# Summing phi(k) over the tiles by strided reductions on the Vector engine instead of column-tiled matmuls

## The chip, the cores and the metric

The kernel runs on one core of a Trainium2 chip. The metric is the device time of one execution in microseconds (us). A profile is one execution taken by the hardware profiler; its span is about 2 us shorter than the time. TensorE (PE) does the matmuls, PEld is its weight load, DVE is the Vector engine, ACT the Scalar engine, POOL GpSimd. The granted clock is the share of TensorE's full clock that the throttle let through.

## The reference, cut to what matters

```python
phi = lambda t: jnp.where(t > 0, t + 1, jnp.exp(t)) + 1e-6
pq, pk = phi(q), phi(k)
kv = jnp.einsum("bhsd,bhse->bhde", pk, v)
z = jnp.einsum("bhsd->bhd", pk)                       # sum over all 2048 rows
num = jnp.einsum("bhqd,bhde->bhqe", pq, kv)
den = jnp.einsum("bhqd,bhd->bhq", pq, z)[..., None] + 1e-6
a = (num / den) ... @ wo                              # linear attention, 32 heads of 16
b = mixer_mlp(x)                                      # layernorm, two large matmuls with gelu
out = g * a + (1 - g) * b                             # g: a sigmoid gate per row
```

The change is about `z`, the sum of phi(k) over all rows, which the normalizer `den` needs. phi(k) lies in `pk`, 128 partitions by 16 tiles by 512 channels, bf16. Its 2048 rows are 16 tiles of 128 partitions, so `z` is a sum over the 16 tiles and then over the partitions.

## The kernel before

The sum over the tiles was sixteen matmuls, each 32 columns wide, accumulated in PSUM, issued between steps of another accumulation (`gacc`). Two ops on DVE then split the sum into two bf16 parts, and four small matmuls summed over the partitions.

```python
def z_tile(t):
    g = t % 4
    mm(zacc[32 * g : 32 * g + 32, :], zsel[:], pk[:, t, :], t < 4, t >= NT - 4,
       tile_position=(0, 32 * g))
...
zacc = bank("zacc")
for t in range(NT - LAG, NT):
    g_tile(t)
    if t == NT - 3:
        for u in range(NT):
            z_tile(u)
...
nc.vector.tensor_copy(out=zhi[:], in_=zacc[:])
nc.vector.scalar_tensor_tensor(out=zhl[:], in0=zhi[:], scalar=odd[:], in1=zacc[:], ...)
```

Then come the query steps. Each has three matmuls of the MLP (`uacc`), four of a query block (`qacc`), and on DVE two ops that make phi(q) (`pqT`). After them TensorE works through the other eleven MLP tiles of sixteen matmuls each (j = 3 to 13). In between stand the normalizer's matmuls (`den_matmuls`), and the chain that multiplies `pqT` by one over the denominator (`rden`), 16 multiplications on DVE fed by DMA:

```python
for j in range(NB0, NF):                 # NB0 = 3, NF = 14
    ...                                  # sixteen uacc matmuls, gelu
    if j == NB0:
        den_matmuls()
        rden_chain()
    elif j <= NB0 + ND:
        w2_matmul(j - NB0 - 1)
    ...
```

The output phase follows: for each of 16 tiles four `aps` matmuls and fourteen `yps` matmuls.

## Time and profile before

| | before |
|---|---|
| time, median of 3 runs | 168.21 us (167.87 to 168.40) |
| span of the profile | 166.4 us |
| TensorE busy, granted clock | 97%, 0.998 |
| DVE busy | 48% |

The first lines are from the page: busy times with their share of the span and the instructions, and then the span in 40 slices of 4.2 us, each digit the busy share of one slice in tenths (9 is 90% or more); PEclk is the granted clock in the same tenths.

```profile
PE 161.7 (97%) x806; PEld 74.9 (45%) x806; DVE 80.2 (48%) x190; ACT 59.0 (35%) x91; POOL 18.2 (11%) x37
...
PE   7999999999999999999999999999999999999992
...
PEclk9999999999999999999999999999999999999999
```

The next is the chain of work that ended last, by engine:

```profile
PE 94%; DMA 3%; DVE 1%; SPq 0%; issue 0%
```

TensorE's last wait, 0.41 us for a DMA, ends at 6.03 us, and nearly the whole chain is TensorE's. The time is the length of its instruction stream. Now the timeline of TensorE around the sums (start, duration, engine, line, op, out<-in, shape, count), and after the query steps:

```profile
30.24 2.75 PE L109 MATMUL gacc<-pk,xs 128*128 128x512 bf16 x12
32.92 1.05 PE L109 MATMUL zacc<-pk,zsel 128*32 128x512 bf16 x16
33.91 1.90 PE L109 MATMUL gacc<-pk,xs 128*128 128x512 bf16 x8
35.64 0.60 PE L109 MATMUL uacc<-hs,w1c 128*128 128x512 bf16 x2
```

```profile
60.87 3.62 PE L109 MATMUL uacc<-hs,w1c 128*128 128x512 bf16 x16
64.41 1.05 PE L109 MATMUL denps<-pqT,Z 128*32 128x512 bf16 x16
```

From start to start, the sums and the last gacc steps fill 30.24 to 35.64 us. An MLP tile with the tiling switch after it takes 64.41 - 60.87 = 3.54 us.

DVE in one query step (the bracket is the idle time in front and what ended it):

```profile
52.63 0.29 DVE L208 TENSOR_SCALAR e<-e 128x512 bf16<-128x512 bf16 x1 [0.49 <-ACT e L207]
52.96 0.69 DVE L211 SCALAR_TENSOR_TENSOR pqT<-qacc,e 128x512 bf16<-128x512 f32 x1
54.14 0.29 DVE L208 TENSOR_SCALAR e<-e 128x512 bf16<-128x512 bf16 x1 [0.49 <-ACT e L207]
```

A step comes every 1.51 us; DVE works for about one of it and waits 0.49 us for ACT. This looks like room for a reduction of half a microsecond or a little more.

### The profile page before, as it was taken

The page shows a single profiled execution, that of the slowest core. Times are in us where ns is not written, and L with a number is a line of the kernel's source. Part 1 is how long each engine was busy: PE and PEld are TensorE (multiplying, and loading weights), DVE is VectorE, ACT ScalarE, POOL GpSimd, SP SyncE. Part 2 cuts the span into 40 slices and gives each one's busy share as a digit, 9 for nine tenths or more (in the row PEclk, how much of TensorE's full clock was granted, in tenths as well). Part 3 has the DMA queues.
Part 4 walks back from the last instruction along what each step waited for, and adds up shares of the span by engine and source line. Part 5 has one row for each costly group of instructions (what it writes and reads, how often), then busy time and mean ns, then how long its engine had stood idle before and what let it go on. Part 6 is the DMA issues. An engine that isn't in the chain of part 4 may idle for free.

```text
span 166.4 us, 2105 instructions
## 1 busy us (share of the span) xinstructions
PE 161.7 (97%) x806; PEld 74.9 (45%) x806; DVE 80.2 (48%) x190; ACT 59.0 (35%) x91; POOL 18.2 (11%) x37
## 2 busy tenths in 40 slices
PE   7999999999999999999999999999999999999992
PEld 3544444444544444444444444444444444444461
DVE  1569999986986769992301504051222121111121
ACT  3272474827658557222222111051111222111110
POOL 5000602100020000002712521000000000000000
PEclk9999999999999999999999999999999999999999
DMA  5999999999700001910597499931100000110001
GB/s 155 257 181 274 345 352 347 348 349 338 186 0 2 0 0 55 357 33 32 188 293 194 140 336 274 313 127 64 35 32 32 32 33 32 47 51 32 32 32 32
DMA packets 28953, 24.78 MB, mean 149 GB/s; under 512 B 6736, under 2 KB 28368, under 8 KB 28944
## 3 DMA queue, kind: packets, MB, share of 16 engines
q1 hardware_dynamic: 26928, 21.76, 45.0%
q0 software_dynamic: 1440, 2.38, 5.0%
q10 hardware_dynamic: 576, 0.52, 1.0%
q8 instruction: 6, 0.10, 0.3%
q14 instruction: 3, 0.02, 0.0%
HBM read 21.11 MB, written 2.23 MB: 140 GB/s over the span
## 4 chain that ended last, share of the span: by engine, by line
PE 94%; DMA 3%; DVE 1%; SPq 0%; issue 0%
PE uacc L109 29%; PE yps L109 29%; PE gacc L109 8%; PE qacc L109 8%; PE aps L109 8%; PE kacc L109 8%; DMA wk_sb<-in_A_wqkv_dram 3%; PE zacc L109 1%; PE denps L109 1%; PE kvps L109 1%; PE wps L109 1%; SPq L125 0%; DVE ot L471 0%; PE pt L197 0%; DVE xT L203 0%
## 5 line engine op out<-in xcount | busy, mean ns | idle before, releaser
L109 PE MATMUL uacc<-hs,w1c 128*128 128x512 bf16 x224 | 52.0, 379 | 0.0
L109 PE MATMUL yps<-uT,w2c 128*128 128x512 bf16 (+1 forms) x238 | 51.0, 367 | 0.0
L109 PEld LDWEIGHTS <-w2c 128*128 128x128 bf16 x238 | 23.3, 98 | 25.3
L109 PEld LDWEIGHTS <-w1c 128*128 128x128 bf16 x224 | 21.7, 98 | 26.3 <-issue 0.4
L471 DVE SCALAR_TENSOR_TENSOR ot<-yps,c,a_sc 128x512 bf16<-128x512 f32 (+1 forms) x17 | 12.1, 719 | 42.2 <-PE yps L109 41.2
L456 ACT ACTIVATE a_sc<-aps,c,gg 128x512 f32<-128x512 f32 x16 | 12.3, 777 | 46.8 <-PE aps L109 38.9
L418 DVE TENSOR_TENSOR pqT<-pqT,rex 128x512 bf16<-128x512 bf16 x16 | 6.6, 425 | 26.6 <-DMA rex<-rd_dram 26.5
L337 ACT ACTIVATE uT<-uacc,bcol 128x512 bf16<-128x512 f32 x14 | 9.3, 687 | 27.5 <-PE uacc L109 27.5
L109 PE MATMUL kacc<-wk_sb,xT 128*128 128x512 bf16 x64 | 16.1, 379 | 0.5 <-DMA wk_sb<-in_A_wqkv_dram 0.4
L109 PE MATMUL aps<-W2sb,pqT 128*128 128x512 bf16 x64 | 16.4, 379 | 0.0
L109 PE MATMUL qacc<-xT,wq_sb 128*128 128x512 bf16 x64 | 16.4, 379 | 0.0
L109 PE MATMUL gacc<-pk,xs 128*128 128x512 bf16 x64 | 16.1, 380 | 0.0
L247 ACT ACTIVATE hs<-xs,nmr,rstd 128x512 bf16<-128x512 bf16 x16 | 12.8, 804 | 2.5 <-DVE nmr L241 2.5
L207 ACT ACTIVATE e<-qacc 128x512 bf16<-128x512 f32 x16 | 9.6, 597 | 10.2 <-PE qacc L109 10.2
L207 ACT ACTIVATE e<-kacc 128x512 bf16<-128x512 f32 x16 | 9.1, 593 | 8.9 <-PE kacc L109 8.9
L208 DVE TENSOR_SCALAR e<-e 128x512 bf16<-128x512 bf16 x32 | 9.1, 284 | 6.3 <-ACT e L207 6.3
L211 DVE SCALAR_TENSOR_TENSOR pk<-kacc,e 128x512 bf16<-128x512 f32 x16 | 11.1, 692 | 0.6
L211 DVE SCALAR_TENSOR_TENSOR pqT<-qacc,e 128x512 bf16<-128x512 f32 x16 | 11.1, 692 | 0.5
L416 POOL DMA_DIRECT2D rex<-rd_dram x16 | 9.4, 597 | 16.6 <-DVE pqT L418 14.9
L231 DVE BATCH_NORM_STATS2 stats<-xs 128x6 f32<-128x512 bf16 x16 | 10.9, 682 | 0.0
L404 DVE CUSTOM_DVE_ANT_0 junk<-xs,gw_b 128x512 bf16<-128x512 bf16 x16 | 9.9, 688 | 0.0
L109 PEld LDWEIGHTS <-xT 128*128 128x128 bf16 x64 | 6.1, 98 | 8.2 <-issue 0.9
(66 smaller groups left out, 67.6 us busy)
## 6 DMA issues: line engine op xcount, KB each, us to landing
w2c<-in_B_w_dram SPq DMA_DIRECT2D x4, 1792.0 KB, 9.8
w1c<-in_B_w_dram SPq DMA_DIRECT2D x2, 2048.0 KB, 16.1
w1c<-in_B_w_dram SPq DMA_DIRECT2D x3, 1024.0 KB, 11.3
rex<-rd_dram POOLq DMA_DIRECT2D x16, 128.0 KB, 6.6
out_dram<-ot SPq DMA_DIRECT2D x15, 128.0 KB, 1.7
xs<-in_A_x_dram SPq DMA_DIRECT2D x2, 512.0 KB, 4.0
xs<-in_A_x_dram SPq DMA_DIRECT2D x2, 256.0 KB, 4.4
wq_sb<-in_A_wqkv_dram SPq DMA_DIRECT2D x1, 512.0 KB, 6.0
```

What stands on the lines that cost most here:

```text
L109: nc.tensor.matmul(o, lhsT=lhsT, rhs=rhs, start=start, stop=stop, **kw)
L207: nc.scalar.activation(out=e[:], in_=acc[:], func=ACT.Exp)
L208: nc.vector.tensor_scalar(out=e[:], in0=e[:], scalar1=1.0, scalar2=PHI_EPS, op0=ALU.min, op1=ALU.add)
L211: nc.vector.scalar_tensor_tensor(out=dst, in0=acc[:], scalar=0.0, in1=e[:], op0=ALU.max, op1=ALU.add)
L231: nc.vector.bn_stats(out=stats[:], in_=xs[:, t, :])
L247: nc.scalar.activation(out=hs[:, t, :], in_=xs[:, t, :], func=ACT.Identity, scale=rstd[:, t : t + 1], bias=nmr[:, t : t + 1],)
L337: nc.scalar.activation(out=uT[:, j, :], in_=acc[:], func=ACT.Gelu_apprx_tanh, bias=bcol[:, j : j + 1])
L404: nc.vector.tensor_tensor_reduce(out=junk[:], in0=xs[:, t, :], in1=gw_b[:], scale=1.0, scalar=0.0, op0=ALU.mult, op1=ALU.add, accum_out=gp ...
L416: nc.gpsimd.dma_start(out=rex[:], in_=src.unsqueeze(1).to_broadcast([8, HEAD, SC]))
L418: nc.vector.tensor_tensor(out=seg, in0=seg, in1=rex[:], op=ALU.mult)
L456: nc.scalar.activation(out=a_sc[:], in_=aps[:], func=ACT.Identity, scale=gg[:, t : t + 1], bias=c2[:, t : t + 1],)
L471: nc.vector.scalar_tensor_tensor(out=ot[:, :W], in0=yps[:, :W], scalar=c1[:, t : t + 1], in1=a_sc[:, cs], op0=ALU.mult, op1=ALU.add,)
```

## The change

Its intent is to take the sixteen matmuls off the engine that bounds the kernel and put the sum on DVE, which has time. Sixteen reductions each sum 32 channels over the 16 tiles. Ten stand in query steps 6 to 15, six after them. As the sum is ready later, the matmuls of the normalizer go two MLP tiles later.

```diff
-    def z_tile(t): ...                       # sixteen column-tiled matmuls
+    def z_sum(i):
+        d = slice(i * 32, (i + 1) * 32)
+        nc.vector.tensor_reduce(
+            out=zacc[:, d], in_=pk[:, :, d].rearrange("p t d -> p d t"), op=ALU.add, axis=AX.X
+        )
 ...
+    def z_split():
+        nc.vector.tensor_copy(out=zhi[:], in_=zacc[:])
+        nc.vector.tensor_tensor(out=zlo[:], in0=zacc[:], in1=zhi[:], op=ALU.subtract)
+    def z_matmuls(): ...                     # eight small matmuls (zps) instead of four, then Z32
 ...                                          # in the query steps:
+        if t >= 6:
+            z_sum(t - 6)
 ...                                          # after them:
+    for i in range(10, 16):
+        z_sum(i)
+    z_split()
 ...                                          # in the MLP tiles:
-        if j == NB0:
-            den_matmuls()
-            rden_chain()
-        elif j <= NB0 + ND:
-            w2_matmul(j - NB0 - 1)
+        if j == NB0 + 1:
+            z_matmuls()
+        if j == NB0 + 2:
+            den_matmuls()
+            gate_sums()                      # 16 DVE ops, before: in front of the reciprocal
+            rden_chain()
+        if NB0 + 3 <= j < NB0 + 3 + ND:
+            w2_matmul(j - NB0 - 3)
```

The innermost dimension of each reduction's input is `t`, so two elements that are read one after the other lie 512 bf16 values, 1024 bytes, apart.

More of the change, by code (lines that the diff above doesn't have):

```diff
@@ L83 @@
     zhi = keep([P, D], BF16, "zhi")
-    zhl = keep([P, D], BF16, "zhl")
-    odd = keep([P, 1], FP32, "odd")
-    neg8 = keep([P, 8], BF16, "neg8")
-    zsel = keep([P, 32], BF16, "zsel")
+    zlo = keep([P, D], BF16, "zlo")
+    zacc = keep([P, D], FP32, "zacc")
+    ones8 = nc.const_aps.tensor(1.0, (P, 8), BF16)
     rden = keep([P, SC], BF16, "rden")
@@ L162 @@
     nc.vector.memset(Z32[:], 0.0)
-    nc.vector.memset(zsel[:], 0.0)
-    nc.vector.memset(zsel[:, 0:2], 1.0)
-    nc.vector.memset(neg8[:], -1.0)
     nc.gpsimd.memset(ident[:], 0.0)
@@ L170 @@
     )
-    nc.vector.tensor_reduce(out=odd[:], in_=ident[:, 1:P:32], op=ALU.add, axis=AX.X)
     block_mask(mask[:].rearrange("p (a b) -> p a b", b=HEAD), P // HEAD, HEAD)
@@ L268, in q_block @@
         phi(pqT[:, j, c * SC : (c + 1) * SC], qacc)
-    def z_tile(t):
-        g = t % 4
-        mm(
-            zacc[32 * g : 32 * g + 32, :], zsel[:], pk[:, t, :], t < 4, t >= NT - 4,
-            tile_position=(0, 32 * g),
+    def z_sum(i):
+        d = slice(i * 32, (i + 1) * 32)
+        nc.vector.tensor_reduce(
+            out=zacc[:, d], in_=pk[:, :, d].rearrange("p t d -> p d t"), op=ALU.add, axis=AX.X
         )
@@ L315 @@
             ln_shift(t // TPC - 2)
-    zacc = bank("zacc")
     for t in range(NT - LAG, NT):
         g_tile(t)
-        if t == NT - 3:
-            for u in range(NT):
-                z_tile(u)
     ln_shift(2)
     ln_apply(NT - APPLY)
-    nc.vector.tensor_copy(out=zhi[:], in_=zacc[:])
-    nc.vector.scalar_tensor_tensor(
-        out=zhl[:], in0=zhi[:], scalar=odd[:], in1=zacc[:], op0=ALU.mult, op1=ALU.subtract
-    )
     gT = persist.tile([P, ND, D], BF16, name="gT", tag="wk_sb")
@@ L357, in kv_matmuls, with z_matmuls @@
         )
+    def z_split():
+        nc.vector.tensor_copy(out=zhi[:], in_=zacc[:])
+        nc.vector.tensor_tensor(out=zlo[:], in0=zacc[:], in1=zhi[:], op=ALU.subtract)
+    def z_matmuls():
         zps = bank("zps")
         for j in range(ND):
-            mm(zps[:, 8 * j : 8 * j + 8], zhl[:, j * P : (j + 1) * P], neg8[:], True, True)
+            for i, part in enumerate((zhi, zlo)):
+                mm(
+                    zps[:, 8 * j : 8 * j + 8], part[:, j * P : (j + 1) * P], ones8[:],
+                    i == 0, i == 1,
+                )
         nc.vector.tensor_tensor(
@@ L398, with gate_sums @@
             kv_matmuls()
+        if t >= 6:
+            z_sum(t - 6)
     for jj in range(NB0):
         gelu(jj, accs[jj])
-    for t in range(NT):
-        junk = work.tile([P, D], BF16, name="junk", tag="junk", bufs=2)
-        nc.vector.tensor_tensor_reduce(
-            out=junk[:], in0=xs[:, t, :], in1=gw_b[:], scale=1.0, scalar=0.0,
-            op0=ALU.mult, op1=ALU.add, accum_out=gpre[:, t : t + 1],
-        )
+    for i in range(10, 16):
+        z_sum(i)
+    z_split()
+    def gate_sums():
+        for t in range(NT):
+            junk = work.tile([P, D], BF16, name="junk", tag="junk", bufs=2)
+            nc.vector.tensor_tensor_reduce(
+                out=junk[:], in0=xs[:, t, :], in1=gw_b[:], scale=1.0, scalar=0.0,
+                op0=ALU.mult, op1=ALU.add, accum_out=gpre[:, t : t + 1],
+            )
     def rden_chain():
```

## The prediction

> **What bounds the kernel now.** TensorE. The page gives it 97% of the 166.4 us span at full clock; the chain of waits is 94% TensorE with no gap after the first microseconds. So the time is the length of TensorE's stream, plus any new wait put into it. DVE is 48% busy.
>
> **What leaves that stream.** In the timeline gacc's slot ends at about 32.83 us, sixteen zacc matmuls start at 32.92, gacc again at 33.91: 1.08 us with the switch into and out of column tiling. They hide no wait: pk of the last tile is written by 33.50 and the last gacc step would need it at 33.69, a thin margin. The four zps matmuls after kvps (44.15 to 44.25) go too: 0.1 us. The query loop should end 1.18 us earlier, at 59.7 instead of 60.87.
>
> **What it adds.** Eight small zps matmuls after the second MLP tile: about 0.3 us with their start behind a wait. On DVE 16 strided reductions and a split, less the zhi and zhl pair (1.4 us).
>
> **Cost of one reduction.** No trace has this shape. The four-element reduction took 159 ns; [...] ops of 512 elements here (bn_stats, gate sums) start 0.61 us apart. I estimate 0.61 us. [...] The danger is the stride: each element is 1024 bytes from the next. [...]
>
> **Is it on the critical path?** In query steps DVE spends 0.33 + 0.61 us and idles 0.49 per 1.515 us (timeline). With a reduction: 1.55, so DVE falls behind by 0.04 a step, 0.4 us after ten. The query accumulators' five banks absorb that. The last pqT ends near 61.8; seven reductions end near 66.1; cast and subtraction (dependent, 1.2 us) near 67.4. TensorE reaches the zps matmuls at 59.7 + 2 x 3.47 = 66.6. So I expect a new wait there of 0.8 us, which gives back most of the gain:
> -1.18 + 0.3 + 0.8 = -0.1 us.
>
> If the stride halves the rate (1.15 us each), lag grows to 5 us, the split ends near 76, TensorE waits 9 us: about 176.5 us. In between (0.8 us): a wait of 3.7 us, about 171 us.
>
> **Later.** den moves to the end of the third tile, near 72 us; reciprocal then starts about when it does now (72.4, where it waits behind the gate sums). The gate sums now stand before the rden multiplications: the first moves from 81.0 to about 85.6, the last (108.6) by 0 to 4 us. The first a_sc waits for c2 behind them; free banks cover this until about 115: no cost expected.
>
> **Prediction.** 168.3 us, 80% range 167.0 to 172.5. Faster by over 2%: 1%; within 2%: 77%; slower by over 2%: 22%.
>
> **What would show it right.** Groups: reductions about 0.69 us busy, zacc matmuls gone. Timeline: query phase starts near 34.6 without a TensorE gap; DVE steps without idle time. Waits: TensorE's weight load of zlo waits on the DVE subtraction, 0.3 to 1.5 us, before the third MLP tile; no other new wait.
>
> **What would make it wrong.** Reductions above 0.85 us (slower by over 2%), or faster than 0.55 us (no wait, about 167.4 us). A lag that empties the query banks. A stall at the last gacc step. An rden chain that runs past 115 us and starves the output phase.

The forecast's sum, -1.18 + 0.3 + 0.8, came to -0.1 us, and the forecast to 168.3 us. The 0.61 us that the sum rests on is the start-to-start time of other ops of 512 elements (0.68 and 0.69 us busy in the profile before). The 1.15 and 0.8 us of the other scenarios are suppositions.

## The result

| | before | changed |
|---|---|---|
| time, median of 6 runs | 168.43 us | 175.42 us (174.58 to 176.26) |
| ratio of the fast runs, 95% interval | | 1.0424 (1.0376 to 1.0473) |
| span of the profile | 166.4 us | 174.2 us |
| granted clock of the profiled run | 0.998 | 0.979 |

One run of the kernel before, 170.44 us, is over 1.5% above its fastest and so counts as slow: the ratio is 175.44 us, the changed kernel's mean, over 168.30, the mean of the other five. A ratio is the mean time of one kernel's fast runs over that of the other's of the same rounds, so it is not quite the ratio of the medians. The change is 4.2% slower, outside the predicted range. The slices of the changed kernel's page, 4.4 us each:

```profile
PE   8899999999999993399999999999999999999992
...
PEclk9999999999999999659999999999999999999999
```

There is a hole in TensorE's row (slices 16 and 17), and the granted clock is 0.6 and 0.5 in slices 17 and 18. The chain runs over DVE for a fifth of the span:

```profile
PE 75%; DVE 19%; DMA 2%; issue 1%; SPq 0%; ACT 0%
```

The gain is there. The timeline of TensorE from the same gacc step to the query steps is 34.84 - 30.53 = 4.31 us, where it was 5.40:

```profile
30.53 4.48 PE L108 MATMUL gacc<-pk,xs 128*128 128x512 bf16 x20
34.84 0.81 PE L108 MATMUL uacc<-hs,w1c 128*128 128x512 bf16 x3
```

The group of the reductions (busy time, mean ns of one, idle before) and then DVE's timeline in a query step and after the last one:

```profile
L267 DVE TENSOR_REDUCE zacc<-pk 128x32 f32<-128x512 bf16 x16 | 15.7, 1017 | 0.0
```

```profile
53.20 0.69 DVE L206 SCALAR_TENSOR_TENSOR pqT<-qacc,e 128x512 bf16<-128x512 f32 x1
53.81 1.03 DVE L267 TENSOR_REDUCE zacc<-pk 128x32 f32<-128x512 bf16 x1
54.76 0.28 DVE L203 TENSOR_SCALAR e<-e 128x512 bf16<-128x512 bf16 x1
...
65.00 6.52 DVE L267 TENSOR_REDUCE zacc<-pk 128x32 f32<-128x512 bf16 x7
71.55 0.43 DVE L346 CAST zhi<-zacc 128x512 bf16<-128x512 f32 x1
72.02 0.69 DVE L347 TENSOR_TENSOR zlo<-zacc,zhi 128x512 bf16<-128x512 f32 x1
```

A reduction is busy for 1.02 us, and the next op starts 0.93 to 0.95 us after it, not 0.61. DVE's idle time is gone and a query step takes it 55.08 - 53.20 = 1.88 us (the next phi multiplication starts at 55.08) against TensorE's 1.51. It is over 3 us late at the last step, needs 6.5 us more for seven reductions, and ends the split at 72.7 us. TensorE:

```profile
59.97 7.07 PE L108 MATMUL uacc<-hs,w1c 128*128 128x512 bf16 x32
72.04 0.19 PE L108 MATMUL zps<-const-bfloat16-1.0,zhi 128*128 128x8 bf16 x1 [5.00 <-DVE zhi L346]
72.77 0.19 PE L108 MATMUL zps<-const-bfloat16-1.0,zlo 128*128 128x8 bf16 x1 [0.54 <-DVE zlo L347]
...
72.98 6.19 PE L108 MATMUL uacc<-hs,w1c 128*128 128x512 bf16 x16
79.10 1.05 PE L108 MATMUL denps<-pqT,Z 128*32 128x512 bf16 x16
```

TensorE comes to the zps matmuls at 67.0 and stands idle for 5.00 us until DVE has written zhi, and for 0.54 us until it has written zlo. The next MLP tile, 72.98 to 79.10, takes 6.12 us instead of 3.54. The busy times by stretches of 1 us (the third number from the right is the granted clock) show why:

```profile
core 0: us, PE busy (x) PEld busy (x) DVE busy (x) ACT busy (x) POOL busy (x), PEclk, DMA share, GB/s
...
70.00:71.00 1.00, 0.00 (x0) 0.00 (x0) 1.00 (x2) 0.00 (x0) 0.00 (x0) 1.00 0.07 18
71.00:72.00 1.00, 0.00 (x0) 0.00 (x0) 0.95 (x2) 0.00 (x0) 0.00 (x0) 0.70 0.00 0
...
74.00:75.00 1.00, 1.00 (x3) 0.30 (x2) 0.00 (x0) 0.00 (x0) 0.00 (x0) 0.50 0.09 16
...
78.00:79.00 1.00, 1.00 (x5) 0.35 (x3) 0.00 (x0) 0.00 (x0) 0.00 (x0) 0.89 0.00 0
```

The clock falls to half during the wait, near 71.4 us (0.70 over that microsecond), stays at 0.50 and comes back near 78.2 us (0.89). So the spans account for themselves:

| from start to start on TensorE | change in us |
|---|---|
| start of the kernel up to gacc (30.24 to 30.53), which no edit touches | +0.29 |
| zacc matmuls gone (5.40 to 4.31) | -1.09 |
| four zps matmuls gone from the query steps | -0.10 |
| from the end of the second MLP tile (59.97 + 2 x 3.45 = 66.87) to the third (72.98): wait, and eight zps matmuls of about 0.2 | +6.11 |
| third MLP tile at the lower clock (3.54 to 6.12) | +2.58 |
| sum; the spans differ by 7.8 | +7.79 |

Two theories are needed, each with a rival. For the slow reduction: **A**, the distance between elements costs, or **B**, each of the 32 outputs costs. For the slow tile: **C**, the clock fell because TensorE stood idle, or its operands were slow. These names are used in the expectations.

### The profile page after: what moved, and what is told of

Read it like the earlier page. It is cut to its first block, busy times and chain, and to the rows that moved or that the text cites. A ratio compares the mean times of both kernels' runs of the same rounds, so it can differ in the third digit from the quotient of the medians.

```text
span 174.2 us, 2092 instructions
## 1 busy us (share of the span) xinstructions
PE 163.9 (94%) x794; PEld 75.6 (43%) x794; DVE 93.7 (54%) x202; ACT 59.0 (34%) x91; POOL 18.2 (10%) x37
## 4 chain that ended last, share of the span: by engine, by line
PE 75%; DVE 19%; DMA 2%; issue 1%; SPq 0%; ACT 0%
PE yps L108 28%; PE uacc L108 21%; DVE zacc L267 9%; PE gacc L108 8%; PE kacc L108 8%; PE aps L108 8%; DVE pqT L206 6%; DMA wk_sb<-in_A_wqkv_dram 2%; DVE e L203 2%; PE qacc L108 1%; DVE stats L226 1%; PE denps L108 1%; PE wps L108 0%; SPq L124 0%; DVE zlo L347 0%
## 5 line engine op out<-in xcount | busy, mean ns | idle before, releaser
L108 PE MATMUL uacc<-hs,w1c 128*128 128x512 bf16 x224 | 54.7, 393 | 0.0
L108 PEld LDWEIGHTS <-w1c 128*128 128x128 bf16 x224 | 22.3, 101 | 28.0 <-issue 3.9
L267 DVE TENSOR_REDUCE zacc<-pk 128x32 f32<-128x512 bf16 x16 | 15.7, 1017 | 0.0
```

Source lines behind the costliest of these rows:

```text
L108: nc.tensor.matmul(o, lhsT=lhsT, rhs=rhs, start=start, stop=stop, **kw)
L267: nc.vector.tensor_reduce(out=zacc[:, d], in_=pk[:, :, d].rearrange("p t d -> p d t"), op=ALU.add, axis=AX.X)
```

## The experiments

Ten kernels were run. Unless said otherwise the result is right. Runs on one chip are compared with the kernel before on that chip, with medians of 168.19 us (e1 to e4) and 168.46 us (e5 to e8, and on a third chip e9 and e10).

### e1_patterns: what does a reduction of 512 elements cost?

```diff
-        nc.vector.tensor_reduce(out=zacc[:, d], in_=pk[:, :, d].rearrange("p t d -> p d t"), ...)
+        # two of each: distance s = 1, 4, 8, 16, 32 elements inside one tile, then the original;
+        x = pk[:, i, :].rearrange("p (g t s) -> p g s t", t=16, s=s)
+        # then one output of 512 adjacent, 256 outputs of 2 adjacent
+        nc.vector.tensor_reduce(out=o, in_=x, op=ALU.add, axis=AX.X)
```

> Wrong result on purpose: the sixteen reductions of 512 bf16 elements read different patterns, two of each, to read their durations. Outputs of 16 elements each with element distances of 2 bytes (sa), 8 (sb), 16 (sc), 32 (sd), 64 (se) and 1024 bytes (sf, the changed kernel's own); one output of 512 adjacent elements (one); 256 outputs of 2 adjacent elements (many); then two strided copies and two additions of a whole tile into fp32. Theory A, the distance between elements costs: sa and sb about 0.69 us busy, sd, se and sf about 1.02, sc on either side. Theory B, each output costs some 10 ns whatever the distance: sa to sf all about 1.02 us, one 0.69, many over 3 us. If A holds, a strided copy costs as much too (about 1.0 us) and the adjacent addition about 0.69.

Durations by tile, in ns (min/median/max), for distances of 8, 16 and 1024 bytes, and for 256 outputs of two adjacent elements:

```profile
L283 DVE TENSOR_REDUCE sb<-pk x2: 676/676/676, 50.1 to 51.6; 128x32 f32<-128x512 bf16 x2
...
L283 DVE TENSOR_REDUCE sc<-pk x2: 1061/1062/1064, 53.1 to 55.0; 128x32 f32<-128x512 bf16 x2
...
L283 DVE TENSOR_REDUCE sf<-pk x2: 1019/1024/1028, 63.5 to 64.6; 128x32 f32<-128x512 bf16 x2
...
L283 DVE TENSOR_REDUCE many<-pk x2: 676/681/686, 66.8 to 67.6; 128x256 f32<-128x512 bf16 x2
```

The edit also puts two strided copies and two additions behind the reductions, and takes one of the four output buffers (`opool`) away, as e10 does. The distance of 2 bytes took 678 ns, those of 32 and 64 bytes 1062 and 1008, the single output 680, a strided copy 585. Theory A holds and B falls: 256 outputs cost no more than one (681 and 680 ns), while at 16, 32, 64 and 1024 bytes 512 elements take 0.33 to 0.39 us more than at 2 or 8. One expectation was wrong: a copy with the same distance took only 0.58 us. e10 follows that up.

### e2_contiguous: the same reductions without the distance

```diff
-            out=zacc[:, d], in_=pk[:, :, d].rearrange("p t d -> p d t"), op=ALU.add, axis=AX.X
+            out=zacc[:, d], in_=pk[:, i, :].rearrange("p (d t) -> p d t", t=NT), op=ALU.add, axis=AX.X
```

> Wrong result on purpose: the same sixteen reductions with the same 32 outputs each, but over adjacent elements of one tile. Theory A (distance costs): each 0.69 us busy, 0.61 from start to start, TensorE's wait before the third MLP tile shrinks from 5.5 to about 0.8 us, the following MLP tile takes 3.5 us, and the time is about 168.3 us, what the prediction said for the whole change. Theory B (outputs cost): nothing changes, 175.4 us.

The reductions of this run:

```profile
L267 DVE TENSOR_REDUCE zacc<-pk x16: 674/676/680, 47.7 to 64.9; 128x32 f32<-128x512 bf16 x16
```

167.81 us, ratio 0.9981 (0.9963 to 0.9999), granted clock 1.00 in the profile; TensorE's wait was 0.31 us. It sums wrong elements, which the comparison with the reference did not notice, so it says nothing about correctness. With the distance alone taken away, the whole loss is gone. The order of work, the wait's place and the extra DVE work are the same as in the changed kernel.

### e3_fill: the same wait, with TensorE kept busy

```diff
     def z_matmuls():
+        fill = bank("fill")
+        for _ in range(25):
+            mm(fill[:], warm[:, 0:P], warm[:], True, True)
         zps = bank("zps")
```

> Right result: 25 idle matmuls on constants (5.4 us at 0.216 each) stand between the second MLP tile and the zps matmuls, so that TensorE works through the time in which it waited; the zps matmuls start no later. Theory C (the clock granted to TensorE fell because it stood idle for 5 us): the third MLP tile takes 3.5 us in place of 6.2, granted clock 1.00, and the time is about 172.7 us. Rival (its operands or its weight loads were slow, whatever stood before): it takes 6.2 us still, 175.4 us.

```profile
66.14 5.63 PE L108 MATMUL fill<-const-bfloat16-1.0 128*128 128x512 bf16 x25
...
72.22 3.61 PE L108 MATMUL uacc<-hs,w1c 128*128 128x512 bf16 x15
75.76 1.05 PE L108 MATMUL denps<-pqT,Z 128*32 128x512 bf16 x16
```

173.07 us, ratio 1.0292 (1.0275 to 1.0308). The zps matmuls wait for the same split, and the tile after them takes 75.76 - 72.22 = 3.54 us, as in the kernel before; the granted clock is 1.00. Useless work made the changed kernel about 2.3 us faster (medians of different rounds). The slow tile was due to the idle time, not to its operands.

### e4_late: the normalizer later, after the split has ended

```diff
-        if j == NB0 + 1:
+        if j == NB0 + 3:
             z_matmuls()
-        if j == NB0 + 2:
+        if j == NB0 + 4:
             den_matmuls()
```

The W2 matmuls follow two tiles later as well.

> Right result: the zps matmuls two MLP tiles later (after the fourth, when the split has long ended), den and the W2 matmuls two tiles later too. If the whole loss is the wait and the clock that follows it: no wait, no slow tile, and the gain that the prediction read from TensorE's stream is left, 1.18 us less 0.2 for four more zps matmuls: about 167.4 us, ratio 0.994. If the later rden chain starves the output phase, or DVE's lag costs anything else: 169 us or more with a TensorE gap past 110 us.

168.50 us, ratio 1.0016 (0.9989 to 1.0043). The wait, the slow tile and the 4% are gone, but the gain of 1 us was not left, and the expectation missed. The first aps matmul starts at 99.82 us, 0.98 before that of the kernel before, but TensorE then waits in the output phase (TensorE's line with the gap in its bracket, then DVE):

```profile
116.19 1.02 PE L108 MATMUL aps<-W2sb,pqT 128*128 128x512 bf16 x4 [0.66 <-ACT a_sc L461]
```

```profile
113.63 1.26 DVE L420 TENSOR_TENSOR pqT<-pqT,rex 128x512 bf16<-128x512 bf16 x3 [1.93 <-DMA rex<-rd_dram]
...
115.09 0.18 DVE L453 TENSOR_TENSOR c<-c,bcol 128x16 f32<-128x16 f32 x1
```

The values `c2` that the first output needs stand on DVE behind all sixteen multiplications of the rden chain. They come at 115.3 us. By then four outputs have been started, each with two of the eight buffers of the program's PSUM pool (`bufs=8`), so the fifth finds none free; that the buffers are what it waits for is read from the bracket, not tested. In the kernel before, the last multiplication started at 108.58 us, and in the changed one at 113.13, where the outputs also began later.

### e5_wait2: a shorter wait

The edit is that of e4, with `NB0 + 2` and `NB0 + 3`.

> Right result: the zps matmuls, den and W2 one MLP tile later than in the changed kernel. The split ends at the same time, so TensorE should wait 5.5 less 3.5, about 2.0 to 2.3 us. Theory C in its strict form (a wait of 5 us lets the clock fall, a wait of about 2 us is too short): granted clock 1.00, the tile after the wait takes 3.5 us, and the time is 167.5 + 2.2, about 169.7 us. If any wait lets the clock fall: the tile after it takes about 6 us and the time is about 172.4 us.

TensorE's timeline, then the stretches of 1 us:

```profile
71.69 0.18 PE L108 MATMUL zps<-const-bfloat16-1.0,zhi 128*128 128x8 bf16 x1 [1.60 <-DVE zhi L346]
72.42 0.18 PE L108 MATMUL zps<-const-bfloat16-1.0,zlo 128*128 128x8 bf16 x1 [0.55 <-DVE zlo L347]
...
72.61 5.30 PE L108 MATMUL uacc<-hs,w1c 128*128 128x512 bf16 x16
77.84 1.05 PE L108 MATMUL denps<-pqT,Z 128*32 128x512 bf16 x16
```

```profile
72.00:73.00 1.00, 0.58 (x9) 0.39 (x10) 0.55 (x2) 0.00 (x0) 0.00 (x0) 1.00 0.00 0
73.00:74.00 1.00, 1.00 (x6) 0.40 (x5) 0.00 (x0) 0.00 (x0) 0.00 (x0) 0.90 0.07 16
...
77.00:78.00 1.00, 1.00 (x8) 0.34 (x10) 0.00 (x0) 0.06 (x1) 0.00 (x0) 0.89 0.00 0
```

171.63 us, ratio 1.0197 (1.0176 to 1.0218). The wait was 2.15 us and the clock still fell, in all four runs (granted clock 0.988 to 0.990). So the strict form of theory C, in which only a wait of some 5 us counts, is wrong. The tile took 5.23 us, 1.69 too many. The clock fell near 73.8 us, over a microsecond after TensorE had taken up its work, and came back near 77.2.

So the clock stood at half for 3.4 us here (73.8 to 77.2) and for 6.8 us in the changed kernel (71.4 to 78.2). Why it fell only after TensorE had taken up its work here, and within the wait there, no run shows. The price was not fixed by the length of the wait either: with waits of 5.9 us in e1, 5.5 in the changed kernel and 5.6 in e8, at mean clocks of 0.98, 0.979 and 0.98, the tile after the wait lost 1.6, 2.6 and 2.8 us (it took 5.14, 6.12 and 6.30). The changed kernel's profile is that of the slowest of its six runs.

### e6_late_gates: c2 in front of the last eight multiplications

```diff
+        if j == NF - 2:
+            gates()                          # tanh on ACT, gg, c1, c2 on DVE
+            rden_chain(rd_dram, (2, 3))      # the last eight multiplications
```

The rest is e4_late, with only the first eight multiplications issued after den.

> Right result: e4_late, with the gate's tanh and the three small DVE ops that make c2 moved in front of the last eight rden multiplications, which only the ninth output tile and later ones need. Theory D (e4_late lost its gain because c2 stood behind all sixteen multiplications and came at 115 us, 15 us after the first aps matmul): the TensorE gap at 116 us goes, and the time is 1 us below before, about 167.4 us, ratio 0.994. Rival (the gain is not there): 168.2 to 168.5 us again.

168.05 us, ratio 0.9975 (0.9952 to 0.9999). `c2` was now there at 103 us and the gap of 0.66 us went, but another of 0.41 us came, and the expected 167.4 us was not reached. The waits of TensorE:

```profile
PE yps L108 <- DVE ot L485: 0.4, 1, 0.4
```

The outputs' own DVE op (`ot`) still stands in line with the multiplications, which stand in front of it in DVE's stream and wait for their DMA until after 115 us. Theory D is half right: `c2` was one part, the late chain itself another.

### e7_adds: adjacent additions, and a version to beat both

```diff
-    def z_sum(i): ...
+    def z_add(t):
+        nc.vector.tensor_tensor(
+            out=zacc[:], in0=pk[:, 0, :] if t == 1 else zacc[:], in1=pk[:, t, :], op=ALU.add
+        )
 ...
+        if t >= 6:
+            z_add(t - 5)
 ...
+    for i in range(11, 16):
+        z_add(i)
 ...
+        if j == NB0 + 2:
+            z_matmuls()
+        if j == NB0 + 3:
+            den_matmuls()
```

The gates stand as in e6.

> Right result, meant to beat both kernels: the sums are fifteen additions of a whole tile of adjacent elements into fp32, ten of them in the query steps, in place of the strided reductions; zps matmuls after the third MLP tile (j = 5), den after the fourth, gates in front of the last eight multiplications as in e6_late_gates. Additions 0.69 us busy, 0.70 from start to start when they follow each other; the split ends near 67.5 us, before TensorE comes to it at 70; no TensorE wait anywhere: about 167.4 us, ratio 0.994 to 0.995. If DVE's lag in the query steps or the chain of rden hurts: 168 us or more.

```profile
L266 DVE TENSOR_TENSOR zacc<-zacc,pk x14: 680/681/694, 49.8 to 65.6; 128x512 f32<-128x512 f32 x14
```

167.61 us, ratio 0.9954 (0.9940 to 0.9968). An addition starts 0.60 us before the next op in a query step, a step takes DVE 1.53 us, the split ends at 67.5 us, and TensorE comes to the zps matmuls at 70.4. Nothing in its stream waits from the query steps to the end. This is faster than the kernel before by 0.5%, and that is about all there was to win: 1.19 us less 0.2 for the zps matmuls.

### e8_patterns2: what else costs?

Each reduction is replaced by one of the patterns that the expectation names.

> Wrong result on purpose, to read more durations, two of each: a reduction with elements 12 bytes apart (fa, 480 elements); reductions over groups of 2, 4 and 8 adjacent elements, the groups 1024 bytes apart (fb, fc, fd, 512 elements each); an addition of two operands with 1024 bytes between elements (into zhi); an addition with one such operand (into zacc); an addition of adjacent operands that writes 16 bytes apart (into zlo); an adjacent addition into fp32. [...] fb, fc and fd are near 0.68 us and fa is between 0.65 and 1.0; if every jump costs, fb is near 0.85, fc near 0.77, fd near 0.72. If the cost is that of the read and not of the reduction, both strided additions take 1.02 us or more.

By tile: pairs of adjacent elements 1024 bytes apart, and an addition that writes 16 bytes apart:

```profile
L277 DVE TENSOR_REDUCE fb<-pk x2: 677/677/677, 51.1 to 52.7; 128x16 f32<-128x512 bf16 x2
...
L289 DVE TENSOR_TENSOR zlo<-pk x2: 2426/2426/2427, 65.1 to 67.6; 128x512 bf16<-128x512 bf16 x2
```

Groups of 4 and 8 adjacent elements took 676 ns as well, and elements 12 bytes apart (480 of them) 798 ns; an addition took 1036 with one operand 1024 bytes apart, and as much with both, where e7's additions of adjacent elements took 681. So the distance in what is read costs in an addition as in a reduction. In a reduction, pairs of adjacent elements 1024 bytes apart took no longer than 512 adjacent ones (677 and 680 ns), as the first form of the expectation said. A pattern that was not expected to be dear is: writing 16 bytes apart took 2.43 us.

### e9_adds_early: e7 with the normalizer one tile earlier

The edit is that of e7, with `NB0 + 1` and `NB0 + 2`.

> Right result: e7_adds with the zps matmuls, den and W2 one MLP tile earlier, where the changed kernel has them. The split ends near 67.5 us and TensorE comes to the zps matmuls near 66.7 to 66.9, so it waits about 0.7 us. Waits of 0.3 to 0.7 us have left the clock at 1.00 (e2, e3, e4) and one of 2.2 us has not (e5). If the clock stands: about 168.3 us, 0.7 over e7_adds, granted clock 1.00. If it falls: about 170 us.

```profile
67.22 0.18 PE L108 MATMUL zps<-const-bfloat16-1.0,zlo 128*128 128x8 bf16 x1 [0.47 <-DVE zlo L346]
```

168.21 us, ratio 0.9977 (0.9943 to 1.0012). TensorE waited 0.47 us and the clock stayed at 1.00. The runs spread from 167.31 to 168.37, and in the profiled one the start waited 1.2 us for a DMA instead of 0.4, so the comparison of times is inconclusive. What the profile shows is that a wait of half a microsecond left the clock alone: the tile after it took 3.55 us. With the 1.2 us at the start the mean clock of the run was 1.00 as well. No wait between 1.2 us and the 2.15 of e5 was run.

### e10_copies: why is the strided copy not slower?

The first six reductions are replaced by copies of 32 x 16 elements and 31 x 16 elements 1024 bytes apart, and of adjacent elements; the others are left out.

> Wrong result on purpose, to read durations, two of each: in e1_patterns a plain copy of 512 bf16 elements 1024 bytes apart took 0.58 us, not 1.0. [...] A copy of 32 x 16 such elements (into zhi) should again take about 0.58 us; one of 31 x 16, whose destination is 496 adjacent elements (into wide), should take about 1.0 us[...], and about 0.57 if copies are just not slowed; a copy of 512 adjacent elements (into zlo) about 0.27.

```profile
L271 DVE COPY zhi<-pk x2: 595/596/596, 47.9 to 49.3; 128x512 bf16<-128x512 bf16 x2
...
L271 DVE COPY wide<-pk x2: 1003/1004/1004, 50.8 to 52.7; 128x496 bf16<-128x496 bf16 x2
```

The adjacent copy took 285 ns. The copy of 31 x 16, which has fewer elements, takes 1.00 us, and that of 32 x 16 takes 0.60. So copies pay for the distance as well, 0.60 or 1.00 us instead of 0.285, and how much depends on the pattern. Why 32 x 16 costs less than 31 x 16, no run shows.

## Why the prediction was wrong

- **Right: what bounds the kernel, and what the matmuls cost.** 1.08 us was predicted for the zacc matmuls and 1.09 measured; the thin margin at the last gacc step held.
- **Wrong: the cost of one reduction.** This is the step that failed: "I estimate 0.61 us". It measured 0.93 us from start to start (1.02 busy); the prediction had named a reduction above 0.85 us among the things that would make it wrong. The estimate took the per-element rate of ops that read adjacent elements (bn_stats, gate sums) for one that reads elements 1024 bytes apart. e1 and e2 show that the distance is the whole difference: 0.68 us with adjacent elements, and a kernel at 167.8 us. The 0.69 us busy that the prediction looked for was right for adjacent elements (0.68 us in e1 and e2). By itself this step brings about 173 us: e3, where the time of the wait passed but the clock held, measured 173.07.
- **The warning was there.** The prediction called the distance of 1024 bytes the danger, priced it in two scenarios, and gave 22% to a change slower by over 2%. The profile before has no op of this shape. e1 and e8 measured it: 0.68 us at 8 bytes, 1.06 at 16, 1.02 at 1024, and 0.68 for pairs of adjacent elements 1024 bytes apart.
- **Right: how that would move the wait.** The arithmetic of lag, tail and wait was sound. With 0.8 us it gave a wait of 3.7 us and with 1.15 us one of 9; at 0.93 it measured 5.5. At 0.61, the size that e2's adjacent elements have, it gave 0.8 and e2 measured 0.31. The query accumulators' banks absorbed even the lag of over 3 us: TensorE has no gap in the query steps.
- **Missing: the clock.** Every scenario priced a wait on TensorE at its own length. The wait of 5.5 us cost 2.6 us more in the tile after it in the profiled run (e3 shows that it was the idle time), and one of 2.15 us cost 1.7 more (e5).
- **Right: "Later".** The gate sums in front of the multiplications and the late chain cost nothing: TensorE waits for nothing in the output phase of the changed kernel. There it was late itself, so this alone would not show that the reasoning was sound; the first multiplication came at 93.2 us, not 85.6. But in e2 the order is the same and TensorE was on time: the first multiplication came at 84.7 us, the last at 109.9 and `c2` at 110.7, and TensorE did not wait there either. In e4, where the normalizer stands two tiles later than in the changed kernel, `c2` came at 115.3 us, at the limit of 115 that the prediction named, and most of the gain was lost (0.66 of 0.98 us).

## What to carry to other kernels

Before moving a sum to DVE, look at which dimension is innermost in what it reads: adding whole tiles of adjacent elements gave the same sum at 0.68 us an op instead of 1.02. When an engine that is off the critical path gets new work, follow it to the place where the bound engine next needs it, and charge a long wait of TensorE with more than its length: here waits of 2.15 us and of over 5 us cost 1.6 to 2.8 us on top, at the lower clock after them. And when a chain is moved later, check what stands behind it in the same engine's queue.
